# Performer attention and two expert layers on one core: attention's products in float32 on halves of the matrix array, two pairs of heads at a time

## The chip, the cores and the metric

The kernel runs on one core of one Trainium2 chip. The core has a matrix engine (PE; its weight loads are shown as PEld), a vector engine (DVE), a scalar engine (ACT), a general engine (POOL) and a queue engine (SP) that issues the transfers. The metric is the time of one execution on the device, in microseconds (us), lower is better: 965.58 us, the median of 3 runs (965.34 to 966.15).

## The reference

Four batches, 8 heads, 576 positions, 64 values per head; 128 random features `omega`. The attention is linear (features instead of a softmax over positions), then two expert layers follow, each with 2304 tokens of 512 values.

```python
def phi(x):                                    # x is q or k, scaled
    proj = np.einsum('bhsd,md->bhsm', x, omega)
    h = proj - np.sum(x * x, axis=-1, keepdims=True) / 2.0
    h = h - np.max(h, axis=-1, keepdims=True)
    return np.exp(h) / np.sqrt(m)
kv = np.einsum('bhsm,bhsd->bhmd', k_p, v)      # key sums
z = np.sum(k_p, axis=2)
num = np.einsum('bhsm,bhmd->bhsd', q_p, kv)    # numerators
den = np.einsum('bhsm,bhm->bhs', q_p, z)[..., None] + 1e-06
attn = num / den
# layer 1: silu(x @ w_gate) * (x @ w_val) @ w_out;  layer 2: squared, clipped (x @ w_in) @ w_out
```

## The kernel before

The program is written by a planner (`Planner`): each piece of work is a coroutine that yields operations (`Op`) with an engine and an assumed cost, waits for events, and takes buffers from rings. The planner walks through this in assumed time and emits the instructions; each engine runs its own in that order, and semaphores keep the dependencies. Where an operation may run on more than one engine, `pl.pick` takes the one that is free first by the plan. PE, DVE and ACT instructions of different coroutines are so interleaved by priorities (`PR_K`, `PR_Q`, `PR_C` and others).

There are eight PSUM banks of 128x512 (`bank`). Precision is that of float32: the expert layers write each operand as a high and a low part in a rounded format (`parts`, L411) and multiply three times (`split3`, L415 to 418). Attention does its products in one of two ways. In full float32 one product is two instructions on PE. In the split form an operand's high and low part are made by DVE, ACT or POOL, and a product is three instructions.

- Keys come in 36 groups (`k_group`) of two tiles of 128 positions, for a pair of heads. The pair's 64 values each stand above each other on the 128 rows of the array, and `omr` (128x256) is `omega` twice, on the diagonal, with zeros elsewhere. `front` (L620) makes the squares (`squares`), the projection, the maximum over 128 features, and the exponent. The first 26 key groups and the first 17 query groups (`NATP`) use float32 (L632), the others `split3` with `xhl` and `omh`, `oml`.
- Key sums (L705): for each tile and head one product of the 128 features with 128 columns: 64 values and 64 columns of ones, so that the sum `z` stands 64 times. `kv_evac` brings them to SBUF, as `kvr` in float32, and as `kvz` in two parts.
- Queries come in nine blocks of 256 positions and four pairs of heads (`q_group`). The features are transposed on PE (L790) to `qtn` or, split, to `qt` (L802). `num` multiplies: the first three blocks (`NATK`) in float32 on column halves of the array (L894), two heads side by side, numerators and denominators in one bank; the others split (L902). `norm_whole` and `norm_halves` divide: DVE transposes the denominators in 32x32 blocks, takes reciprocals of one column, and transposes back (L819 to 827, L838 to 860).
- The result `os` becomes a tile `x1s` in two parts (`x1_split`) and goes to DRAM. Expert steps of layer 1 begin when both halves of a block are there. Weights arrive as 64-bit numbers and are converted by one ACT and four DVE operations each (`to_f32`, L433 to 440), 68 of them in all.

A bank is returned when the last reader of it has been planned; a coroutine that asks for a bank waits in the plan.

Of the kernel before, what the change touches and what calls it, by code (L numbers as in the profile page):

```python
# [28 lines left out]
P = 128  # L29
# [15 lines left out]
SLACK_A = 0.0  # L45

O_OFF, P_OFF, H_OFF = 32, 48, 48

NATK = 3

SQ3 = True

NATP = 26

N_2 = 0

NWL, NB1 = 7, 8
KINS, VINS, QINS, EBK, EBQ, N_QT = 3, 5, 2, 4, 2, 3
N_KL, N_VL = 3, 0
# [10 lines left out]
PR_K0, PR_K, PR_Q0, PR_Q = 0.32, 1.04, 0.17, 0.83  # L70
PR_C0, PR_C, PR_CS = 0.66, 1.20, 1.10
# [4 lines left out]
N_GATE, N_CS = 2, 3  # L76
# [206 lines left out]
def performer_moe_kernel(ctx: ExitStack, tc: tile.TileContext, qG, kG, om, ident,  # L283
# [59 lines left out]
    stat = ring(att, "st", 10, [P, 4, 4])  # L343
    rec = ring(att, "rec", 2, [P, TB])
    rect = ring(att, "rect", 1, [P, TB // 32, 33])
    vin = ring(att, "vi", VINS, [P, 576])
    qts0 = ring(att, "qtn", 3, [P, 2, TB])
    qts = ring(att, "qt", N_QT, [P, 2, 2, TB], F32R)
    ids = att.tile([P, P], F32, name="ids")
    omr = att.tile([P, 256], F32, name="omr")  # L350
    omh = att.tile([P, 256], F32R, name="omh")
    oml = att.tile([P, 256], F32R, name="oml")
    pad(att, "pada", 64)
    ebufs = {False: ring(att, "ebk", EBK, [P, 512]), True: ring(att, "ebq", EBQ, [P, 512])}
    kin = ring(att, "ki", KINS, [P, 512])
    qin = ring(att, "qi", QINS, [P, 512])
    nat_b = sorted({b for b in range(4) for k in range(NATK) if b * 576 < (k + 1) * TB and k * TB < (b + 1) * 576})
    kvr = {(b, d): att.tile([P, 2, 2, P], F32, name=f"kvr{b}_{d}") for b in nat_b for d in range(2)}
    xhl = ring(att, "xhl", 2, [P, 2, 256], F32R)
    kvz = [[att.tile([P, 2, 2, 2, P], F32R, name=f"kvz{b}_{d}") for d in range(2)] for b in range(2)]  # L360
# [21 lines left out]
    lend(kin, "kl", N_KL, [P, 512])  # L382
    lend(vin, "vl", N_VL, [P, 576])
    lend(qin, "ql", 2, [P, 512])
    lend(ebufs[False], "el", 2, [P, 512])
# [194 lines left out]
    q_done = {(k, d): Ev() for k in range(NBLK) for d in range(2)}  # L580
# [3 lines left out]
    omr_ready, om_ready, ids_ready = Ev(), Ev(), Ev()  # L584

    def prep():
        yield from dma(omr, om, 131072)
        yield Op("ACT", c_act(256), lambda: nc.scalar.activation(omr, omr, AF.Copy, scale=scale))
        pl.set(omr_ready)
        yield Op("ACT", c_act(256), lambda: nc.scalar.activation(omh, omr, AF.Copy))  # L590
        yield Op("DVE", c_dve(256), lambda: nc.vector.tensor_tensor(out=oml, in0=omr, in1=omh.bitcast(F32), op=ALU.subtract))
        pl.set(om_ready)
        yield from dma(ids, ident, 65536)
        pl.set(ids_ready)

    def squares(x, sq, x_ev):

        if x_ev is not None:
            yield x_ev
        how = pl.pick(ACT=0.96, DVE=c_act(256) + c_dve(256))  # L600
        if how == "ACT":
            def acc4():
                for u in range(4):
                    xu = x[:, u * 64:(u + 1) * 64]
                    nc.scalar.activation(xu, xu, AF.Square, scale=0.25, accum_out=sq[:, u:u + 1])
            yield Op("ACT", 0.96, acc4)
        else:
            yield Op("ACT", c_act(256), lambda: nc.scalar.activation(x, x, AF.Square, scale=0.25))
            yield Op("DVE", c_dve(256), lambda: nc.vector.tensor_reduce(
                out=sq, in_=x.rearrange("p (u d) -> p u d", u=4), axis=AX.X, op=ALU.add))  # L610

    def margin():
        if moe_on.done and SLACK_A:
            yield SLACK_A
# [247 lines left out]
    def num(k, p, q_t):  # L862
# [53 lines left out]
        if q_cnt[k, d] < 2:  # L916
            return
# [829 lines left out]
```

## Time and profile before

| what | value |
|---|---|
| median of 3 runs | 965.58 us (965.34 to 966.15) |
| the profiled execution | 963.52 us |
| its span | 961.7 us |
| PE busy | 945.6 us (98%) |
| DVE busy | 824.1 us (86%) |
| ACT busy | 567.1 us (59%) |
| POOL busy | 96.8 us (10%) |
| PE clock granted | 1.00 |

The span is what the trace covers from the first to the last instruction; the execution's own time is 1.8 us longer. Busy time counts from an instruction's start to its end, and PE's instructions overlap by some 0.16 us, so the distance between two starts tells what one costs. Idle time of an engine that nothing waits for costs nothing.

### The profile page before, as it was taken

The page shows a single profiled execution, that of the slowest core. Times are in us where ns is not written, and L with a number is a line of the kernel's source. Part 1 is how long each engine was busy: PE and PEld are TensorE (multiplying, and loading weights), DVE is VectorE, ACT ScalarE, POOL GpSimd, SP SyncE. Part 2 cuts the span into 40 slices and gives each one's busy share as a digit, 9 for nine tenths or more (in the row PEclk, how much of TensorE's full clock was granted, in tenths as well). Part 3 has the DMA queues.
Part 4 walks back from the last instruction along what each step waited for, and adds up shares of the span by engine and source line. Part 5 has one row for each costly group of instructions (what it writes and reads, how often), then busy time and mean ns, then how long its engine had stood idle before and what let it go on. Part 6 is the DMA issues. An engine that isn't in the chain of part 4 may idle for free.

```text
span 961.7 us, 21166 instructions
## 1 busy us (share of the span) xinstructions
PE 945.6 (98%) x8094; PEld 927.5 (96%) x8094; DVE 824.1 (86%) x1695; ACT 567.1 (59%) x1490; POOL 96.8 (10%) x99
## 2 busy tenths in 40 slices
PE   8999999999999999999989999999999999999998
PEld 7789899999999999999989999999999999999998
DVE  7999899888999999999989999999889768867553
ACT  8999788887755545455544466564545455544331
POOL 0322246533300000000000000000000000000000
PEclk9999999999999999999999999999999999999999
DMA  8765646645478556574666583336423041303022
GB/s 301 253 198 183 200 154 219 197 140 173 166 241 256 161 190 207 189 248 153 198 206 220 173 277 123 116 125 232 126 73 122 1 143 45 132 1 111 1 89 88
DMA packets 90677, 154.67 MB, mean 161 GB/s; under 512 B 8528, under 2 KB 42320, under 8 KB 90576
## 3 DMA queue, kind: packets, MB, share of 16 engines
q1 hardware_dynamic: 90576, 153.32, 48.7%
q8 instruction: 63, 1.03, 0.4%
q14 instruction: 38, 0.31, 0.1%
HBM read 110.30 MB, written 42.99 MB: 159 GB/s over the span
## 4 chain that ended last, share of the span: by engine, by line
PE 64%; DVE 9%; DMA 7%; ACT 5%; issue 2%; SPq 1%; DVEq 0%; ACTq 0%
PE bank L416 21%; PE bank L418 20%; PE bank L417 20%; DMA ws<-in_w_dram 2%; DMA ws<-in_wo_dram 2%; DMA xq<-x1d 2%; PE bank L902 1%; SPq L390 1%; DVE x1s L409 1%; DMA wtr<-w32o 1%; PE bank L705 1%; PE bank L790 1%; DVE wt L440 1%; ACT rec L838 1%; DVE wt L438 1%
## 5 line engine op out<-in xcount | busy, mean ns | idle before, releaser
L416 PE MATMUL bank<-x1s,w 128*128 128x256 f32 x492 | 138.3, 281 | 0.7 <-DVE eb L1318 0.6
L417 PE MATMUL bank<-x1s,w 128*128 128x256 f32 x492 | 136.2, 277 | 0.0
L418 PE MATMUL bank<-x1s,w 128*128 128x256 f32 x492 | 136.2, 277 | 0.0
L416 PEld LDWEIGHTS bank<-x1s,w 128*128 128x128 f32 x492 | 92.5, 188 | 1.2 <-DVE eb L1318 0.8
L417 PEld LDWEIGHTS bank<-x1s,w 128*128 128x128 f32 x492 | 92.5, 188 | 0.0
L418 PEld LDWEIGHTS bank<-x1s,w 128*128 128x128 f32 x492 | 92.4, 188 | 0.0
L397 ACT ACTIVATE x1s<-xq 128x512 fp32r<-128x512 f32 x81 | 50.8, 628 | 56.0 <-DVE xq L409 27.9
L416 PE MATMUL bank<-x1s,wx 128*128 128x256 f32 x278 | 77.4, 279 | 4.0 <-ACT eb L397 2.6
L416 PE MATMUL bank<-x1s,wb 128*128 128x256 f32 x286 | 79.2, 277 | 0.0
L418 PE MATMUL bank<-x1s,wb 128*128 128x256 f32 x286 | 79.0, 276 | 0.0
L417 PE MATMUL bank<-x1s,wb 128*128 128x256 f32 x286 | 79.0, 276 | 0.0
L418 PE MATMUL bank<-x1s,wx 128*128 128x256 f32 x278 | 76.9, 277 | 0.0
L417 PE MATMUL bank<-x1s,wx 128*128 128x256 f32 x278 | 76.8, 276 | 0.0
L433 ACT ACTIVATE wt<-ws 128x512 f32<-128x512 f32 x68 | 45.8, 676 | 43.9 <-DMA ws<-in_w_dram 22.8
L409 DVE TENSOR_TENSOR x1s<-xq,x1s 128x512 fp32r<-128x512 f32 x90 | 61.4, 684 | 8.4 <-ACT x1s L397 8.1
L397 ACT ACTIVATE eb<-bank 128x512 f32<-128x512 f32 x95 | 55.9, 589 | 19.7 <-PE bank L418 19.3
L397 ACT ACTIVATE hlr<-hb 128x512 fp32r<-128x512 f32 x53 | 33.5, 632 | 49.8 <-PE bank L417 35.2
L416 PEld LDWEIGHTS bank<-x1s,wx 128*128 128x128 f32 x278 | 52.2, 188 | 4.8 <-ACT eb L397 3.3
L651 DVE TENSOR_REDUCE st<-bank 128x4 f32<-128x512 f32 x72 | 48.7, 684 | 8.7 <-PE bank L632 3.9
L416 PEld LDWEIGHTS bank<-x1s,wb 128*128 128x128 f32 x286 | 53.7, 188 | 0.1
L418 PEld LDWEIGHTS bank<-x1s,wb 128*128 128x128 f32 x286 | 53.7, 188 | 0.0
L417 PEld LDWEIGHTS bank<-x1s,wb 128*128 128x128 f32 x286 | 53.7, 188 | 0.0
(281 smaller groups left out, 3610.0 us busy)
## 6 DMA issues: line engine op xcount, KB each, us to landing
ws<-in_w_dram SPq DMA_DIRECT2D x40, 512.0 KB, 4.8
ws<-in_wo_dram SPq DMA_DIRECT2D x28, 512.0 KB, 5.1
xq<-x1d SPq DMA_DIRECT2D x36, 256.0 KB, 5.0
xq<-x2d SPq DMA_DIRECT2D x36, 256.0 KB, 4.1
qi<-in_qG_dram SPq DMA_DIRECT2D x34, 256.0 KB, 3.1
ki<-in_kG_dram SPq DMA_DIRECT2D x33, 256.0 KB, 3.6
vi<-in_kG_dram SPq DMA_DIRECT2D x28, 192.0 KB, 3.5
x1d<-os SPq DMA_DIRECT2D x18, 256.0 KB, 3.2
```

The costliest lines, as they stand in the source:

```text
L390: yield Op("SP", 0.06, lambda: nc.sync.dma_start(dst, src))
L397: yield Op("ACT", c_act(n), lambda: nc.scalar.activation(dst, src, AF.Copy, scale=1.0 if scale is None else scale))
L409: yield Op("DVE", c_dve(n), lambda: nc.vector.tensor_tensor(out=dst, in0=a, in1=b, op=op), True)
L416: nc.tensor.matmul(ps, l_hi, r_hi, start=first, stop=False, skip_group_check=shared)
L417: nc.tensor.matmul(ps, l_hi, r_lo, start=False, stop=False, skip_group_check=shared)
L418: nc.tensor.matmul(ps, l_lo, r_hi, start=False, stop=last, skip_group_check=shared)
L433: yield Op("ACT", 0.575, lambda: nc.scalar.activation(t, hw.bitcast(F32), AF.Abs))
L438: yield Op("DVE", c_dve(512), lambda: nc.vector.scalar_tensor_tensor(out=ti, in0=lw, scalar=29, in1=ti, op0=ALU.logical_shift_right, op1=A ...
L440: yield Op("DVE", c_dve(512), lambda: nc.vector.scalar_tensor_tensor(out=ti, in0=hw, scalar=0xC0000000, in1=ti, op0=ALU.bitwise_and, op1=A ...
L651: yield Op("DVE", c_dve(512), lambda: nc.vector.tensor_reduce(out=st[:, :, 0], in_=psv, axis=AX.X, op=ALU.max, negate=True))
L705: nc.tensor.matmul(kp[:, 2 * pr + a], e[:, u * P:(u + 1) * P], vb[:, vi + (dv if li == 4 else 0), a * 64:a * 64 + P], start=(li == 0 and a ...
L790: nc.tensor.transpose(tp[:, (a * 2 + t) * P:(a * 2 + t + 1) * P], e[:, u * P:(u + 1) * P], ids)
```

## The change

All products of attention are full float32, and the parts of operands (`xhl`, `omh`, `oml`, `kvz`, the two layers of `qt`) are gone. Keys are taken in five groups per batch, one of a single old group and four of two (`GROUPS`), queries two pairs of heads at a time, 18 groups.

- Projections: `omega` stands twice, on rows 0 to 63 and on rows 64 to 127. Each head of a pair is a product of 64 rows on its own half, with its own bank, alternating. 
- Key sums: the 128 features are cut into two halves of 64, each written to its half of the bank's partitions, with 65 columns (64 values and one of ones). `kv_evac` spreads that one column over 64 when it copies.
- Numerators and denominators: always on column halves, for two pairs of heads in one call, in two banks. One `norm` of 512 columns takes the place of `norm_whole` and `norm_halves`.
- Two banks are taken together (`bank_pair`), by one coroutine at a time. Loads are cut into two halves; values are loaded with 130 columns a tile instead of 192. Priorities and ring sizes change.

The number of instructions that the engines get changes so: PE 7354 rows to 7579, DVE 1685 to 1531, ACT 989 to 879. The diff, cut to its core:

```diff
-KINS, VINS, QINS, EBK, EBQ, N_QT = 3, 5, 2, 4, 2, 3
-N_KL, N_VL = 3, 0
+KINS, VINS, QINS, EBK, EBQ, N_QT = 3, 5, 2, 6, 4, 3
+N_KL, N_QL, N_EL = 2, 1, 2
+
+GROUPS = ((0,), (1, 2), (3, 4), (5, 6), (7, 8))
...
+    halves = slice(0, 64), slice(64, P)
+
+    def bank_pair():
+
+        tok = yield Get(two_banks)
+        b0 = yield Get(bank)
+        b1 = yield Get(bank)
+        pl.put(two_banks, tok)
+        return b0, b1
...
+    def front(xb, n, loads, is_q, res, rng):
 
         st = yield Get(stat)
...
-            def proj():
-                for t in range(2):
-                    nc.tensor.matmul(ps[:, t * 256:(t + 1) * 256], xt[:, t * P:(t + 1) * P], omr, start=True, stop=True)
-            yield from margin()
-            yield Op("PE", 0.86, proj)
...
-            yield from parts(hl[:, 0], hl[:, 1], xt, 256)
...
-            def proj():
-                for t in range(2):
-                    split3(ps[:, t * 256:(t + 1) * 256], hl[:, 0, t * P:(t + 1) * P], hl[:, 1, t * P:(t + 1) * P],
-                           omh, oml, True, True)
...
+        banks = yield from bank_pair()
+
+        def proj():
+            for u in range(2 * n):
+                for a, h in enumerate(halves):
+                    nc.tensor.matmul(banks[a][:, u * P:(u + 1) * P], xb[h, 0, u * P:(u + 1) * P], omr[h], start=True, stop=True,
+                                     skip_group_check=True)
+        yield Op("PE", 0.446 * n + 0.1, proj)
...
+        pv = [ps[:, 0:256 * n].rearrange("p (u m) -> p u m", m=P) for ps in banks]
+        for a in range(2):
+            yield Op("DVE", c_dve(256 * n), lambda: nc.vector.tensor_reduce(
+                out=sv[:, a, units, 0], in_=pv[a], axis=AX.X, op=ALU.max, negate=True))
...
-                        nc.tensor.matmul(kp[:, 2 * pr + a], e[:, u * P:(u + 1) * P],
-                                         vb[:, vi + (dv if li == 4 else 0), a * 64:a * 64 + P],
...
+        def mm():
+            for kp, v, u, pr, li in todo:
+                for a in range(2):
+                    for m, h in enumerate(halves):
+                        nc.tensor.matmul(kp[h, 2 * pr + a, 0:65], es[a][:, u * P + 64 * m:u * P + 64 * m + 64],
+                                         v[:, 65 * a:65 * a + 65], start=(li == 0 and a == 0),
+                                         stop=(li == 8 or (li == 4 and pr == 0)), skip_group_check=True)
+        yield Op("PE", 0.232 * len(todo) + 0.15, mm)
...
     def kv_evac(b, d):
         kb = kv_bank.pop((b, d))
...
+        yield from copy(kz[:, :, 0:64], kp[:, :, 0:64], 256, False, 1.0 / P)
+        yield from copy(kz[:, :, 64:P], kp[:, :, 64:65].to_broadcast([P, 4, 64]), 256, False, 1.0 / P)
         pl.put(bank, kb)
-        pl.set(kv_split[b, d])
...
-                yield Op("DVE", c_dve(512), lambda: nc.vector.tensor_tensor(out=lv, in0=tp, in1=hv.bitcast(F32), op=ALU.subtract))
...
+        x = yield Get(osb)
         rc = yield Get(rec)
...
+        banks = yield from bank_pair()
 
         def mm():
...
+            for r in range(2):
+                for what in range(2):
+                    for b, c0, c1 in cuts:
+                        for a, h in enumerate(halves):
+                            nc.tensor.matmul(banks[what][h, r * TB + c0:r * TB + c1], kvr[b, d][:, r, a, halves[what]],
+                                             q_t[:, r, a, c0:c1], start=True, stop=True, skip_group_check=True)
```

The start of PE's order before, after the warm-up. `ki`, `kl` are keys, `qi` queries, `vi` values, `ebk` and `ebq` the exponentials, `ids` the identity:

```order
L632 MATMUL bank_63<-omr,ki_157 128x256 x2
L632 MATMUL bank_64<-omr,ki_158 128x256 x2
L632 MATMUL bank_65<-omr,ki_159 128x256 x2
L632 MATMUL bank_66<-omr,kl_175 128x256 x2
L632 MATMUL bank_67<-omr,kl_176 128x256 x2
L632 MATMUL bank_69<-omr,qi_160 128x256 x2
L632 MATMUL bank_70<-omr,qi_161 128x256 x2
L632 MATMUL bank_68<-omr,kl_177 128x256 x2
L705 MATMUL bank_63<-vi_135,ebk_151 128x128 x4
```

The same place now, the first rows of each group:

```order
L625 MATMUL bank_63<-omr,ki_155 128x128
L625 MATMUL bank_64<-omr,ki_155 128x128
...
L625 MATMUL bank_65<-omr,ki_156 128x128
L625 MATMUL bank_66<-omr,ki_156 128x128
...
L625 MATMUL bank_67<-omr,ki_157 128x128
L625 MATMUL bank_68<-omr,ki_157 128x128
...
L690 MATMUL bank_66<-vi_135,ebk_145 64x65 x2
L690 MATMUL bank_66<-vi_135,ebk_146 64x65 x2
```

A projection of 256 columns in one bank has become products of 128 columns that alternate between two banks, one for each head; a key sum of 128 partitions has become two of 64.

DVE's order before, in the mixed stage, where two numerators of a split block are divided (`rec` holds denominators, then reciprocals; `st` small columns):

```order
L845 STREAM_TRANSPOSE rect_134<-rec_132 128x8x32
L846 RECIPROCAL st_129<-rect_134 128x8
L848 STREAM_TRANSPOSE rec_132<-st_129 128x256
L399 CAST xhl_167<-qi_161 128x256
L845 STREAM_TRANSPOSE rect_134<-rec_133 128x8x32
L802 TENSOR_TENSOR qt_144<-bank_65,qt_144 128x512
L846 RECIPROCAL st_127<-rect_134 128x8
L802 TENSOR_TENSOR qt_143<-bank_70,qt_143 128x512
L848 STREAM_TRANSPOSE rec_133<-st_127 128x256
L748 SCALAR_TENSOR_TENSOR kvz_1_169<-bank_63,kvz_1_169 128x512
L853 TENSOR_TENSOR os_102<-bank_64,rec_133 64x256
```

And now, one division in the same stage:

```order
L781 STREAM_TRANSPOSE rect_134<-bank_70 128x16x32
L635 TENSOR_REDUCE st_128<-st_128 128x8
L418 TENSOR_SCALAR wt_78<-wt_78 128x512
L783 TENSOR_REDUCE st_124<-rect_134 128x16
L647 TENSOR_TENSOR ebk_150<-bank_66,st_128 128x512
L785 RECIPROCAL st_124<-st_124 128x16
L420 TENSOR_SCALAR wt_78<-wt_78 128x512
L786 STREAM_TRANSPOSE rec_132<-st_124 128x512
L631 TENSOR_REDUCE st_130<-bank_64 128x4
L790 TENSOR_TENSOR os_104<-bank_63,rec_132 128x512
```

The transposes read PSUM directly and are twice as long, and the low parts of `qt`, `xhl` and `kvz` no longer stand between them.

## Rows read from the trace of the kernel before

**Rows 1.** The page, busy time, share of the span and instructions of each engine.
```profile
PE 945.6 (98%) x8094; PEld 927.5 (96%) x8094; DVE 824.1 (86%) x1695; ACT 567.1 (59%) x1490; POOL 96.8 (10%) x99
```

**Rows 2.** Table by stage: stretch, its length, busy us (instructions) by engine, clock, DMA.
```profile
0.00:47.30 47.30, 43.21 (x260) 34.88 (x261) 39.15 (x122) 43.25 (x209) 8.74 (x13) 1.00 0.83 281
47.30:256.10 208.80, 206.18 (x1729) 198.47 (x1728) 185.91 (x472) 175.12 (x644) 83.35 (x83) 1.00 0.57 183
256.10:640.00 383.90, 378.12 (x3306) 376.26 (x3305) 364.38 (x693) 203.91 (x382) 4.66 (x4) 1.00 0.59 192
640.00:961.70 321.70, 318.05 (x2807) 317.85 (x2805) 234.69 (x410) 144.83 (x258) 0.00 (x0) 1.00 0.28 91
```

**Rows 3.** First x1 product, last split numerator: ns min/median/max, first and last start.
```profile
L416 PE MATMUL bank<-x1s,w x492: 276/276/469, 47.3 to 924.9; 128*128 128x256 f32 x164
...
L902 PE MATMUL bank<-qt,kvz x192: 213/276/364, 113.5 to 256.0; 128*128 128x256 f32 x96, 128*128 128x128 f32 x48, 128*128 128x192 f32 x24, 128*128 128x64 f32 x24
```

**Rows 4.** Matrix engine's timeline, float32: start us, us, line, operation, instructions.
```profile
31.28 1.95 PE L705 MATMUL bank<-vi,ebk 128*128 128x128 f32 x16
33.06 1.03 PE L632 MATMUL bank<-omr,ki 128*128 128x256 f32 x4
33.93 1.05 PE L705 MATMUL bank<-vi,ebk 128*128 128x128 f32 x8
```

**Rows 5.** The same at two visits to the column halves; PEld are loads.
```profile
27.05 0.61 PE L705 MATMUL bank<-vi,el 128*128 128x128 f32 x4
27.59 1.95 PE L894 MATMUL bank<-qtn,kvr 128*64 128x256 f32 x16
29.47 0.66 PE L790 MATMUL bank<-ids,ebq 128*128 128x128 f32 x4
...
63.57 0.76 PEld L894 LDWEIGHTS bank<-qtn,kvr 128*64 128x64 f32 x16 [0.17 <-DVE ebk L663]
...
63.57 1.10 PE L894 MATMUL bank<-qtn,kvr 128*64 128x64 f32 x16
64.61 0.70 PE L632 MATMUL bank<-omr,qi 128*128 128x256 f32 x2
```

**Rows 6.** The same, split products of 256 columns one by one.
```profile
700.05 0.28 PE L418 MATMUL bank<-x1s,wx 128*128 128x256 f32 x1
700.16 0.28 PE L416 MATMUL bank<-wb,hlr 128*128 128x256 f32 x1
```

**Rows 7.** Groups up to 262 us: count, busy us, mean ns, idle before.
```profile
L651 DVE TENSOR_REDUCE st<-bank 128x4 f32<-128x512 f32 x72 | 48.7, 684 | 8.7 <-PE bank L632 3.9 <-PE bank L418 2.6 <-PE bank L705 0.8
L654 DVE TENSOR_REDUCE st<-st 128x4 f32<-128x8 f32 x144 | 18.8, 148 | 0.5
L838 ACT ACTIVATE rec<-bank 64x256 f32<-64x256 f32 x48 | 18.2, 379 | 9.0 <-PE bank L902 6.3 <-issue 1.2 <-ACT wt L433 0.7
L802 DVE TENSOR_TENSOR qt<-bank,qt 128x512 fp32r<-128x512 f32 x24 | 16.3, 677 | 3.1 <-ACT qt L397 3.0
L407 POOL TENSOR_TENSOR xhl<-qi,xhl 128x256 fp32r<-128x256 f32 x19 | 13.9, 741 | 24.5 <-ACT xhl L397 15.0 <-DVE xhl L399 9.4
L848 DVE STREAM_TRANSPOSE rec<-st 128x256 f32<-128x256 f32 x24 | 10.6, 441 | 0.6
L845 DVE STREAM_TRANSPOSE rect<-rec 128x256 f32<-128x256 f32 x24 | 10.5, 437 | 3.8 <-ACT rec L838 3.7
L853 DVE TENSOR_TENSOR os<-bank,rec 64x256 f32<-64x256 f32 x24 | 10.1, 419 | 0.7
L858 ACT ACTIVATE os<-bank 64x256 f32<-64x256 f32 x24 | 9.0, 377 | 0.3
L407 POOL TENSOR_TENSOR xhl<-ki,xhl 128x256 fp32r<-128x256 f32 x9 | 7.2, 801 | 19.9 <-ACT xhl L397 18.4 <-DVE xhl L399 1.0 <-DVE rect L845 0.5
L397 ACT ACTIVATE xhl<-qi 128x256 fp32r<-128x256 f32 x17 | 7.1, 418 | 1.2 <-PE bank L417 1.0
L397 ACT ACTIVATE xhl<-ki 128x256 fp32r<-128x256 f32 x8 | 3.4, 433 | 0.0
```

More of the change, by code (lines that the diff above doesn't have):

```diff
@@ L579, in performer_moe_kernel @@
     kv_ready = {k: Ev() for k in kvr}
-    q_done = {(k, d): Ev() for k in range(NBLK) for d in range(2)}
+    two_banks = Ring([0])
     x1_tile = {}
@@ new lines, in expo, with each @@
+        def expo(a):
+            e, ps = es[a], banks[a]
+            if pl.pick(ACT=2 * n * 0.262, DVE=c_dve(256 * n)) == "ACT":
+                def each():
+                    for u in range(2 * n):
+                        nc.scalar.activation(e[:, u * P:(u + 1) * P], ps[:, u * P:(u + 1) * P], AF.Exp, bias=sv[:, a, u, 3:4])
+                yield Op("ACT", 2 * n * 0.262, each)
+                pl.put(bank, ps)
+            else:
+                yield Op("DVE", c_dve(256 * n), lambda: nc.vector.tensor_tensor(
+                    out=e[:, 0:256 * n].rearrange("p (u m) -> p u m", m=P), in0=pv[a],
+                    in1=sv[:, a, units, 3].unsqueeze(2).to_broadcast([P, 2 * n, P]), op=ALU.add))
+                pl.put(bank, ps)
+                yield Op("ACT", c_act(256 * n), lambda: nc.scalar.activation(e[:, 0:256 * n], e[:, 0:256 * n], AF.Exp))
@@ L717, in performer_moe_kernel @@
+        for u in range(2 * n):
+            i = 2 * gs[0] + u
+            if i % 9 == 8:
+                pl.spawn(kv_evac(b, i // 9), pl.cur.prio - 0.1)
+        for e in es:
+            back(ebufs[False], e)
+        for g in gs:
+            back(vin, v_tile[b, g])
     v_ready = {(b, g): Ev() for b in range(4) for g in range(9)}
@@ L810, in q_group @@
-        pl.spawn(num(k, p, q_t), pl.cur.prio - 0.05)
-    halves = slice(0, 64), slice(64, P)
-    def norm_whole(ps, pb, rc, xr):
+                    for t in range(2):
+                        u = 2 * r + t
+                        nc.tensor.transpose(tp[:, (a * 2 + t) * P:(a * 2 + t + 1) * P], es[a][:, u * P:(u + 1) * P], ids)
+            yield Op("PE", 4 * 0.11, trans)
+            left[0] -= 1
+            if left[0] == 0:
+                for e in es:
+                    back(ebufs[True], e)
@@ L816, in norm_whole, with norm @@
+            yield from copy(q_t[:, r].rearrange("p a t -> p (a t)"), tp, 512, False)
+            pl.put(bank, tp)
+        ends = [pl.spawn(turn(r), pl.cur.prio) for r in range(2)]
+        for ev in ends:
+            yield ev
+        pl.spawn(num(k, d, q_t), pl.cur.prio - 0.05)
+    def norm(pn, pd, rc, x):
         tt = yield Get(rect)
         st = yield Get(stat)
-        s8 = st.rearrange("p a b -> p (a b)")
-        yield Op("DVE", 0.36, lambda: nc.vector.transpose(out=tt[:, :, 0:32], in_=ps[:, 1].rearrange("p (n c) -> p n c", c=32)))
```

396 lines of the change are left out of this document (123 added, 273 removed).

## The prediction

> **What bounds the kernel now.** I read the busy line of the page first, then a table by stage, then the matrix engine's own timeline at three places, then the groups of the other engines. The busy line gives the matrix engine 98% of the span and the vector engine 86% [rows 1]; a mean does not say which of them ends last where, so the table by stage decides [rows 2]. I cut it at the first expert product, 47.3 us, and at the last attention product, 256.0 us [rows 3]. Up to 47.3 us matrix, vector and scalar engine are all nearly full (43.2, 39.2 and 43.3 us of 47.3), and nothing but attention runs on the matrix engine. From 47.3 to 256.1 us attention and the first expert steps are mixed: the matrix engine is busy 206.2 of 208.8 us, the vector engine 185.9, the scalar engine 175.1. From 256.1 us on there is expert work only: until 640 us the vector engine is at 364.4 of 383.9 us and the matrix engine idles 5.8 us, later only the matrix engine counts. The change touches the first two stages, so what it is worth is read there: matrix time taken out, as long as the vector engine lets it go.
>
> A busy time hides that matmuls overlap, so prices are distances between starts. A float32 product of 256 columns (two instructions) gives 33.06 to 33.93, 0.87 us for 4, 0.217 each; one of 128 columns gives 31.28 to 33.06, 1.78 us for 16, 0.111 each [rows 4]. A split product's instruction of 256 columns takes 0.11 to 0.12 [rows 6]; I use 0.113.
>
> **The change part by part: the matrix engine.** Before, per instruction:
> - projections: 43 groups in float32, 4 x 0.217 = 0.87 each, 37.3 us; 29 groups split, 6 x 0.113 = 0.68 each, 19.7 us. Together 57.0.
> - key sums: 80 tile products of two heads, two instructions each, 320 x 0.111 = 35.5 us.
> - numerators: 12 calls in float32 on column halves and 24 split ones of 6 or 12 instructions. Two float32 calls in a row, 27.59 to 29.47, take 1.88 us for 16 instructions of 256 columns [rows 5]: 8 pairs at 0.217 are 1.73, so the two halves run side by side and 0.15 is lost on the way in and out. 0.94 x 12 = 11.3, a little more for the cut ones: 12.5. The split ones are 192 instructions x 0.113 = 21.7.
> - transposes: the same 144 on both sides.
> Sum without the transposes: 126.7 us.
>
> After:
> - key sums: 640 instructions of 65 columns, in 320 pairs on column halves. The cut numerator call [rows 5] holds the same thing: 63.57 to 64.61 is 1.04 us for 4 pairs of 192 columns and 4 of 64; take off 0.15 and 4 x 0.16 for 192 columns (0.217 x 3/4) and 0.25 is left, 0.06 a pair. 320 x 0.06 = 19 us, 16 less.
> - numerators: 18 calls of 8 pairs at 0.217, 31.2 us without the way in and out, against 34.2: 3 less.
> - projections: 576 instructions of 128 columns in 288 pairs on row halves. No row of before shows row halves. Between 0.111 a pair (side by side, as the column halves) and 0.222 (one after the other) lies 32 to 64 us. I take 0.111, by the nearest row, which is the column halves': 25 less than 57.
> - changes of tiling: in the order of instructions the engine changes between whole array, row halves and column halves 83 times, before 16 times. A visit to the column halves costs 0.15 inside and about 0.1 ahead of it (the 4 products of 27.05 need 0.44, the next starts after 0.54) [rows 5], 0.25 for two changes. Not counting what is in the 12.5 above: 83 x 0.125 = 10.4. A change straight from row to column halves is not shown; 0 to 0.25 for each of these 23 keeps this term between 7.5 and 13.
> Sum: 19 + 31.2 + 32 + 10.4 = 92.6; 34 us less, between 2 (halves one after the other) and 37.
>
> One rule speaks against the 0.111. Loads of 64 columns come 16 in 0.76 us in the cut call [rows 5], less than 0.05 from load to load, with products running beside. The Trainium skill, "TensorE: Matmul & The Clock Gate", section "LDWEIGHTS (loading the stationary operand)", puts a load at its columns divided by 1.2 in nanoseconds, some 53 for 64 columns, 0.85 us for 16 one after another: the trace's 0.76 says that column halves load side by side. For two row halves the same page would give 107 each, 0.213 a pair if one path carried both. By that the projections would be 61 us and nearly the whole gain of this term gone; by the trace's behaviour on column halves it is 32. That is one of the rivals below.
>
> **The other engines.** Vector engine, to the end of attention [rows 7]: out go the low parts of the transposed queries (24 x 0.677 = 16.3), the half-block norms' transposes and products (10.5 + 10.6 + 10.1) with their 24 reciprocals, the 12 whole norms (two transposes at 0.44 and 8 products at 0.42 among them, some 18 in all), 6 low parts of key sums (4 at 0.68 each). In come 18 norms of 512 columns: two transposes at about 0.71 (0.441 plus 256 columns at the 0.265 that separates 0.419 from 0.684), 16 products at 0.68 and 0.3 of small ones, together 42. The small reductions go from 144 to 76 (-10 at 0.148), the exponent's subtraction on this engine from 27 to 38 (+7.5 at 0.68), the sums of squares grow by 4. Net about -29 us. The scalar engine loses the denominators' and numerators' halves (18.2 + 9.0) and the projections' high parts (7.1 + 3.4 at least), 38 us and more; POOL loses the low parts (13.9 + 7.2). Neither was ahead of the vector engine after 47 us, so I count their gains at nothing.
>
> **Where it lands.** Up to the first expert product attention has to bring the keys of one batch and two blocks of queries through the scalar engine, and this part was float32 before too: its squares and exponentials by head are the same. So the first expert product stays at 47 to 50 us. The matrix engine needs only about 28 us there now (a third of the pairs are ahead of it in the order) against 41: these 13 us turn into idle time. From there 80 us of attention are left instead of 102, 22 less, and the order leaves 33 expert instructions (3.7 us) for later that stood before the end of attention: 256.1 - 22 - 3.7 + 2 (later first product) = 232. By the vector engine: 225.1 us up to 256.1 [rows 2], a share of 88%. Minus 29, plus 11 for five more weight conversions that the order now has ahead of the end of attention (30 against 25, two passes of 0.68 and two near 0.44 each), is 207; at the same share 235, and some 4 us of expert work moved behind takes it to 231. The two answers agree on 232. Behind it: 705.6 + 3.7 - 3 (of the 5.8 us of idle matrix time before 640 us, since five conversions fewer are left where the vector engine is at 95%; 0 to 5.8) = 706.3. Span 938.3. The profiled execution took 963.5 us with a span of 961.7, so 940.1; it lay 2.1 us under the median of the runs shown, which may or may not recur. I forecast 939.
>
> What is late next: in the first 50 us the scalar engine, then vector and matrix engine together. Added waits: a projection and a numerator now need two free banks of eight at once, and a token lets one of them gather at a time; queued behind a waiting projection on the matrix engine is the next expert product, whose own bank is held too. The visible idle time of that stage is 2.6 us [rows 2]; I take no more than that, and 0 to 38 us as its bounds (the slower rival below). Loads are no term: the values shrink from 192 to 130 columns a tile, and the transfers' share is 0.57 in that stage.
>
> **Rivals.**
> - All of the matrix time comes out. If the first 47 us shrink with it, nothing turns idle: 961.7 - 34 - 5 = 923 span, 925. Against: the scalar engine's 43.3 of 47.3 us. Range 924 to 931. 0.10.
> - The vector engine holds the mixed stage: groups twice as large come in bursts, two maxima of 0.684 in a row [rows 7], and the matrix engine runs out of expert products to fill in. 10 to 22 us of the saving lost: 950 to 962. For: a vector share of 88% with no slack shown; against: the expert products. A pair of 65 columns that costs 0.11 instead of 0.06 (+16 us, 955) falls in here too. 0.12.
> - The row halves run one after the other. A third of the 32 us falls into the idle time of the first stage, two thirds come back: 939 + 21 = 960, 955 to 966. For: no row shows them, and the rule on loads; against: column halves load and run side by side. It decides from about 0.2 us a pair. 0.07, of which 0.03 within the bound of no change. It is also what remains if the change does not do what it says.
> - Slower: the second bank. 38 projections and 18 numerators each ask for two banks at once, and a bank comes free after a pass of the vector engine over it, 0.684 us for 512 columns [rows 7], or later where it is the second of two. With one such wait on the matrix engine each time, 56 x 0.684 = 38 us are added: 977. It decides from 0.47 us a time (26 us over 56), where the gain against the median is gone. For: a projection's two banks are held through maximum, sums and exponent, before it was one. Against: the 2.6 us of visible idle time in the mixed stage, and expert products queued between. 0.06.
> - The forecast: 931 to 950, likeliest 939. 0.65.
>
> **How the numbers follow.** Faster by over 0.2% (about 1.9 us, what a measurement of this kernel can tell from no change): 0.65 + 0.10 + 0.12 + 0.04 = 0.91. Within: 0.03. Slower: 0.06. The range of 8 in 10: its lower end 925 is the rival with everything out, its upper end 957 takes in half of the one on the vector engine; the other half, the row halves in a row and the slower one stay outside, 0.19 in all.
>
> **What would show it.** Row-half products in pairs a few ns apart, 0.11 from pair to pair, is the step with most weight; 0.22 there makes the forecast wrong. 65-column pairs at 0.06. The first expert product between 45 and 52 us with the matrix engine idle 10 us and more ahead of it. The last attention product at 225 to 240 us. Behind it 700 to 708 us. A vector engine below 80% with matrix idle time in the mixed stage, ended by waits on banks, would speak for the second rival.

## The result, and the profile after

The changed kernel takes 950.96 us (median of 4 runs, 948.91 to 953.10), the kernel before beside it 965.46 (964.20 to 966.15): a ratio of 0.986 [0.984, 0.988], 14.5 us faster. The forecast was 939, range 925 to 957. The profiled execution took 949.58 us, its span is 947.8 us; the sum behind the forecast had 940.1 and 938.3. So 9.5 us of span are to be found.

The page's busy line of the kernel after, to be laid beside [rows 1]:

```profile
PE 920.2 (97%) x8708; PEld 892.9 (94%) x8708; DVE 799.7 (84%) x1536; ACT 515.2 (54%) x1226; POOL 67.6 (7%) x58
```

The first expert product and the last attention product, columns as in [rows 3], and the table by stage cut there, columns as in [rows 2]:

```profile
L400 PE MATMUL bank<-x1s,w x492: 276/276/388, 53.0 to 911.0; 128*128 128x256 f32 x164
...
L817 PE MATMUL bank<-qt,kvr x384: 219/378/687, 23.2 to 239.4; 128*64 128x256 f32 x96, 128*64 128x64 f32 x32, 128*64 128x192 f32 x32, 128*64 128x128 f32 x32
```
```profile
0.00:53.00 53.00, 40.09 (x508) 31.08 (x508) 45.29 (x110) 45.85 (x184) 11.10 (x14) 0.90 0.82 273
53.00:239.40 186.40, 180.32 (x2057) 164.36 (x2059) 161.77 (x340) 126.39 (x419) 53.88 (x42) 1.00 0.64 206
239.40:640.00 400.60, 395.65 (x3464) 393.50 (x3461) 380.24 (x722) 208.46 (x387) 2.60 (x2) 1.00 0.59 190
640.00:947.80 307.80, 304.12 (x2684) 303.92 (x2682) 212.39 (x366) 134.53 (x238) 0.00 (x0) 1.00 0.23 76
```

Against [rows 2] the mixed stage has lost 22.4 us (208.8 to 186.4), the first stage has become 5.7 us longer (47.3 to 53.0), and what lies behind attention 2.8 us longer (705.6 to 708.4, with 3.7 us of expert products moved there). The first stage's matrix engine idles 12.9 us instead of 4.1; the clock it was granted there is 0.90 of full speed, before 1.00.

The matrix engine's timeline in that stage, where [rows 4, 5] stand for before (start us, us, line, operation, instructions, idle before it and what ended it):

```profile
12.75 3.52 PE L625 MATMUL bank<-omr,qi 64*128 64x128 f32 x32 [3.62 <-DMA qi<-in_qX_dram]
16.20 3.04 PE L690 MATMUL bank<-vi,ebk 128*64 128x65 f32 x88
19.17 2.06 PE L625 MATMUL bank<-omr,kl 64*128 64x128 f32 x32
...
25.04 1.16 PE L625 MATMUL bank<-omr,qi 64*128 64x128 f32 x16
26.13 1.39 PE L690 MATMUL bank<-vi,ebk 128*64 128x65 f32 x40
27.44 1.16 PE L625 MATMUL bank<-omr,qi 64*128 64x128 f32 x16
...
33.08 1.41 PE L625 MATMUL bank<-omr,ki 64*128 64x128 f32 x14 [1.96 <-ACT kvr L381]
37.43 2.08 PE L625 MATMUL bank<-omr,ki 64*128 64x128 f32 x16 [2.94 <-ACT ebq L643]
```

At 25.04 sixteen row-half instructions take 1.09 us to the next start: 8 pairs and the way in and out. Forty of 65 columns take 1.31: 20 pairs, 0.06 each with a change of form. Both prices of the forecast are there. The waits, at 12.75 on a transfer of queries and at 33.08 and 37.43 on banks that the scalar engine still reads, are not what the forecast had priced.

### The profile page after: what moved, and what is told of

It is laid out like the page before. It is cut to its first block, busy times and chain, and to the rows that moved or that the text cites. A ratio compares the mean times of both kernels' runs of the same rounds, so it can differ in the third digit from the quotient of the medians.

```text
span 947.8 us, 21783 instructions
## 1 busy us (share of the span) xinstructions
PE 920.2 (97%) x8708; PEld 892.9 (94%) x8708; DVE 799.7 (84%) x1536; ACT 515.2 (54%) x1226; POOL 67.6 (7%) x58
## 4 chain that ended last, share of the span: by engine, by line
PE 64%; DVE 11%; DMA 6%; ACT 2%; issue 2%; SPq 0%; DVEq 0%; ACTq 0%
PE bank L400 20%; PE bank L401 20%; PE bank L402 20%; DMA ws<-in_w_dram 2%; DMA ws<-in_wo_dram 2%; PE bank L817 2%; DVE x1s L393 1%; PE bank L625 1%; DVE w L393 1%; DVE wt L424 1%; DVE wt L422 1%; DVE hb L1211 1%; PE bank L763 1%; DVE wb L393 1%; DVE xi L393 1%
## 5 line engine op out<-in xcount | busy, mean ns | idle before, releaser
L400 PEld LDWEIGHTS bank<-x1s,wx 128*128 128x128 f32 x278 | 52.2, 188 | 1.4 <-ACT eb L381 1.2
L402 PEld LDWEIGHTS bank<-x1s,wx 128*128 128x128 f32 x278 | 52.2, 188 | 0.8 <-POOL wx L391 0.8
```

Of the source, the lines that this page charges most:

```text
L400: nc.tensor.matmul(ps, l_hi, r_hi, start=first, stop=False, skip_group_check=shared)
L402: nc.tensor.matmul(ps, l_lo, r_hi, start=False, stop=last, skip_group_check=shared)
```

## The experiments

All but the last keep the changed kernel's order of instructions on every engine, apart from what is added, left out or turned round inside a group. The kernel before was run beside each; its medians were 964.1 to 965.6. Times are medians; rows and stages are those of one profiled execution of each kernel.

**The row halves in turn.**

```
-            for u in range(2 * n):
-                for a, h in enumerate(halves):
+            for a, h in enumerate(halves):
+                for u in range(2 * n):
```

> The projections of a group run through one row half first and then through the other, so that neighbouring products share a half and cannot lie beside each other; the order on every other engine is that of the changed kernel. Theory A (row halves lie side by side, and matrix time is what the mixed stage is made of): from start to start 0.11 us for each single product instead of for a pair, 32 us more work; a third of it falls into the idle time of the first 53 us, 20 us and more do not: 970 to 980 us. Rival B (the vector engine holds the mixed stage, matrix time is slack): 951 to 957 us. Rival C (the halves load one after the other anyway and gain nothing): no change, 950 to 952 us.

960.66 us (959.60 to 962.31), 9.7 more than the changed kernel; ratio to before 0.995 [0.993, 0.997]. The same visit as at 25.04, from its timeline, and its stages:

```profile
122.72 1.71 PE L625 MATMUL bank<-omr,ki 64*128 64x128 f32 x16
```
```profile
0.00:57.20 57.20, 47.49 (x509) 37.49 (x509) 46.54 (x110) 46.53 (x183) 11.19 (x14) 0.88 0.76 253
57.20:251.70 194.50, 190.59 (x2059) 175.42 (x2059) 163.07 (x340) 127.26 (x419) 53.36 (x42) 1.00 0.61 197
```

It takes 1.64 us to the next start, at 124.36, against 1.09. Inside one half the single starts are 0.112 us apart, as far as the pairs are when the halves alternate: a product alone costs what a pair costs, so the row halves do run side by side. Alternating is not all or nothing, though. Where the second half follows the first, three products of each still start in pairs, 4 to 6 ns apart, in 19 of the 21 visits of this length that stand alone in the trace: 13 steps of 0.112 instead of 16. Some 120 of the 288 pairs are left in this way, so not 32 but about 19 us of matrix time are added. The matrix engine is busy 17.5 us more (937.7), 7.4 in the first stage and 10.3 in the mixed one; the stages are longer by 4.2 and 8.1, since a part fits into idle time. For both reasons no expectation met it.

**The projections on the whole array**, each head's `omega` beside 64 rows of zeros:

```
-                    nc.tensor.matmul(banks[a][...], xb[h, 0, ...], omr[h], ...
+                    nc.tensor.matmul(banks[a][...], xb[:, 0, ...], omz[:, a], ...
```

> The projections go over the whole array again, each head against omega with zeros on the other head's rows, in the same two banks and the same order. Theory A: 576 instructions at 0.111 are 64 us instead of 32, but the 27 visits to the row halves, at about 0.25 to 0.3 us each, are gone: 24 us more, of which some 8 in the idle first stage: 963 to 970 us, under the kernel with the halves in turn by about 8 us. Rival (changes of tiling cost nothing that shows): equal to the kernel with the halves in turn, 970 to 980 us. Rival B (matrix time is slack): 951 to 957 us.

964.68 us (962.60 to 967.79), 13.7 more, ratio 0.999 [0.998, 1.001]: without row halves the whole change is worth nothing that can be measured. The matrix engine is busy 21.3 us more (941.5), and the time lies in the 963 to 970 of theory A. Sixteen instructions take 1.95 us:

```profile
76.51 1.95 PE L630 MATMUL bank<-omz,ki 128*128 128x128 f32 x16
```

**The key sums on the whole array**, 128 features by 65 columns:

```
-                    for m, h in enumerate(halves):
-                        nc.tensor.matmul(kp[h, 2 * pr + a, 0:65], es[a][:, u * P + 64 * m:u * P + 64 * m + 64], ...
+                    nc.tensor.matmul(kp[:, 2 * pr + a, 0:65], es[a][:, u * P:(u + 1) * P], ...
```

> The key sums keep their 65 columns, but each is one product with all 128 features on the whole array instead of two of 64 on column halves. Theory A (the gain of the key sums is that of the columns, 65 instead of 128, and a load of 128 columns keeps up): 0.06 us from start to start, the same work, and up to 20 visits to the column halves fewer at 0.25 us: 946 to 950 us. Rival (a load of 128 columns takes as long as 128 columns of product, 0.11 us, so the halves are what makes 65 columns pay): 320 x 0.05 = 16 us more, 10 to 15 of them behind the first stage: 960 to 967 us.

967.99 us (961.11 to 970.65, 10 runs), 17.0 more, ratio 1.002 [0.999, 1.005].

```profile
127.00 1.89 PE L689 MATMUL bank<-vi,ebk 128*128 128x65 f32 x16
```

Sixteen instructions of 65 columns on the whole array take 1.8 us to the next start, 0.112 each, as much as those of 128 columns: the columns do not set the pace. The Trainium skill, "TensorE: Matmul & The Clock Gate", section "LDWEIGHTS (loading the stationary operand)", puts a load at its columns divided by 1.2 in nanoseconds, 107 for 128 columns; by that the load sets it, and the 0.112 here agrees. The ten runs differ mostly by the clock: 961.11 at a mean clock of 0.994, 970.65 at 0.984. So some of the 17 us is clock, and the expectation of 960 to 967 is met only by the runs above 0.986.

**The column halves in turn.**

```
+            for m, h in enumerate(halves):
                 for kp, v, u, pr, li in todo:
                     for a in range(2):
-                    for m, h in enumerate(halves):
```

> The loop over the two column halves goes outermost in the key sums: first all products of a group on one half, then all on the other; the same 640 pairs of instructions, the same forms and visits. If the two halves work side by side in the changed kernel (two instructions that start 7 ns apart every 0.055 us), 640 instructions of 0.05 us each go from half to whole: 16 us more for the matrix engine, of which about half comes out as with the projections in turn (17.5 us more busy, 9.7 us more time): 957 to 962. If the matrix engine overlaps them in this order too, or a load of 64 columns and not the 65 columns sets the pace: 950 to 953.

958.61 us (957.62 to 961.84), 7.7 more, ratio 0.994 [0.993, 0.996], as expected; the matrix engine is busy 13.7 us more. The visit of 40 instructions:

```profile
128.80 2.32 PE L690 MATMUL bank<-vi,ebk 128*64 128x65 f32 x40
```

To the next start, at 131.05, it is 2.25 us against 1.31: here too the gain hangs on the alternation, and here too three pairs are left where one half follows the other.

**The maxima over half the features.**

```
-                out=sv[:, a, units, 0], in_=pv[a], axis=AX.X, op=ALU.max, negate=True))
+                out=sv[:, a, units, 0], in_=pv[a][:, :, 0:64], axis=AX.X, op=ALU.max, negate=True))
```

> The maximum is taken over 64 of the 128 features and an absolute value stands in for the exponential, so the result is not attention; the order on every engine is unchanged, and only the vector engine's maxima become shorter, 0.68 to about 0.42 us for 68 of 76, some 18 us in all. Theory B (the vector engine holds the first stage and what is lost in the mixed one): the first expert product 3 us earlier and more, the mixed stage shorter by 5 and more: 938 to 945 us. Theory A (matrix work, changes of tiling and the scalar engine's start hold it): 948 to 952 us.

949.03 us (947.59 to 952.78), the same time. Its mixed stage:

```profile
53.90:240.10 186.20, 180.09 (x2059) 164.17 (x2059) 151.84 (x340) 126.59 (x419) 53.59 (x42) 1.00 0.63 206
```

The vector engine has 9.9 us less to do there and the stage lasts 186.2 us, as the changed kernel's 186.4 with 161.77: it does not hold the mixed stage. Nor did the 5 us taken from it in the first stage bring the first expert product earlier (53.9).

**One visit cut into four, and its control.** A product of one column on the whole array (`small`) is added behind each of the tile products of the key sums, or, in the control, all of them behind the visit.

```
         for kp, v, u, pr, li in todo:
             for a in range(2):
                 ...
+            small(kp, v, u)          # the control: in a loop of its own behind this one
```

> Adds 80 products of one column on the whole array to the key sums, one behind every four (of 320) pairs' products, into a column that nothing reads: each visit to the column halves is cut into four or five, 80 visits instead of 20. To be compared with the kernel that has the same 80 products, all at the end of the 20 visits. If a visit costs 0.25 us of the matrix engine, and this engine sets the time in the stage where attention and expert layers are mixed: 60 x 0.25 = 15 us of work, of which half to all comes out in time: 8 to 15 us more than the kernel beside it. If the change of form is hidden: less than 3 us more than it.

> The 80 products of one column, all behind the key sums' visit of their group: 20 visits as before. By itself 80 x 2 x 0.06 to 0.11 us = 10 to 18 us of work for the matrix engine, of which half to all comes out: 956 to 969.

989.82 us (988.04 to 993.88), the control 967.59 (965.39 to 969.97): 22 us for 60 more visits, more than the 8 to 15 expected. The two timelines:

```profile
121.92 0.45 PE L694 MATMUL bank<-vi,ebk 128*64 128x65 f32 x8
122.30 0.38 PE L687 MATMUL bank<-vi,ebk 128*128 128x1 f32 x2
122.61 0.45 PE L694 MATMUL bank<-vi,ebk 128*64 128x65 f32 x8
```
```profile
124.40 1.15 PE L694 MATMUL bank<-vi,ebk 128*64 128x65 f32 x32
125.48 1.05 PE L687 MATMUL bank<-vi,ebk 128*128 128x1 f32 x8
```

Cut, a tile product with its small one takes 0.69 us from start to start; in the control it is about 0.45 (a quarter of 1.08 - 0.15 for the way in and out, and two times 0.11). So a visit costs 0.24 us, two changes of 0.12, and the 60 visits 14.5 us of matrix time. The time rose by 7 us more than that. The clock fell with it: the three runs of 988.04 to 990.2 had a mean granted clock of 0.983 or 0.984, the control's runs 0.989 to 0.994, and 5 to 11 thousandths of this span are 5 to 11 us of matrix time. No run separated the two.

**The clock of the start.** Eight products of zeros fill the waits on the matrix engine, four ahead of the first query projection and two ahead of each of two key projections.

```
         def proj():
+            for _ in range(fill):
+                nc.tensor.matmul(banks[0], idle[:, 0:P], idle, start=True, stop=True)
```

> Eight more products of zeros (128x512, float32, 0.86 us each at full clock) stand in the start, four ahead of the first query projection and two each ahead of two key projections, where the matrix engine waits for a transfer and for banks; the order of all other instructions is that of the changed kernel. Theory B (the half clock costs time): the granted clock of the start stays at or near 1.00, mean 0.998 or more, and the time falls by 3 to 5, to 946 to 948. Theory A (scalar and vector engine hold the start, so a slower matrix engine there costs nothing): clock up, time 949 to 952. If the fillers are in the way: 952 to 954.

954.57 us (954.13 to 957.42), 3.6 slower. Its timeline:

```profile
8.70 3.70 PE L624 MATMUL bank<-hb 128*128 128x512 f32 x8
12.69 1.16 PE L627 MATMUL bank<-omr,qi 64*128 64x128 f32 x16 [0.29 <-DMA qi<-in_qX_dram]
...
15.24 2.79 PE L692 MATMUL bank<-vi,ebk 128*64 128x65 f32 x88
17.96 2.19 PE L627 MATMUL bank<-omr,kl 64*128 64x128 f32 x32
...
37.09 3.26 PE L624 MATMUL bank<-hb 128*128 128x512 f32 x4 [3.42 <-ACT ebq L645]
40.28 1.52 PE L627 MATMUL bank<-omr,ki 64*128 64x128 f32 x16
```

The clock stayed full up to 36 us, and the key sums started 1.0 us earlier than in the changed kernel (15.24 against 16.20), the next projection 1.2 (17.96 against 19.17). At 37.09 the bank came 0.3 us earlier than at 37.43 there. The rest had gone into a longer wait on the scalar engine: a faster matrix engine is worth next to nothing up to there. The last two fillers stood behind that wait instead of in it, ran mostly at half clock (3.26 us for what takes 1.98 at 30 us) and pushed the projection from 37.43 to 40.28 and the first expert product from 53.0 to 55.9; that is the loss. What the half clock costs behind that wait, from 37 us on, this kernel does not show: it fell there here too (0.72 from 36 to 42 us, against 0.61).

**Transfers or engines, and both.** Three kernels. One leaves out the sums of squares. One keeps them but drops the second copy of keys and queries, which only they use, and takes them of the first copy. One leaves out both. The sum of squares is subtracted from the exponent's argument and added back with the maximum, so it only affects the rounding.

```
-                        nc.scalar.activation(xu, xu, AF.Square, ...)      # no squares
-        return [pl.spawn(dma(xb[:, l, ...], src[:, l], ...), ...) for l in range(2)]
+        return [...]                                                      # one copy: l == 0 alone
```

> Leaves out the sums of squares in attention (the scalar engine's squares and the vector engine's reductions of them); in the exponent's argument the sum of squares is subtracted and then, with the maximum, added back, so that the argument is the same up to rounding. The order on every engine is that of the changed kernel with these instructions missing. To the first expert product this takes 28 us of work from the scalar engine (21.5 with accumulators, 6.5 without) and 6.4 us from the vector engine. Theory A (scalar and vector engine together hold the start): the first expert product comes at 43 to 47 us instead of 53.0, the waits for banks in the start go, and the time is 939 to 945. Theory B (what the start lost is the matrix engine's half clock, and the engines do not hold it): only the idle gaps that let the clock fall get shorter, 946 to 950. Theory C (the transfers hold the start, which are busy 0.97 and more from 6 to 30 us): first product stays at 52 to 54 us, 949 to 952.

> Every group of keys and queries is loaded once instead of twice (the second copy, with positions on the partitions, is used by the squares alone); the squares are taken of the first copy instead, so that they are other numbers, and cancel in the exponent's argument as before. All instructions of the engines and their order stay; only these transfers are missing, some 3.2 MB of the 14.5 MB moved ahead of the first expert product (273 GB/s over 53.0 us). Theory C (transfers hold the start): the first expert product comes at 45 to 50 us, since 3.2 MB take 8 to 10 us at the 310 to 380 GB/s of the start, and below some 47 us the 45 to 46 us of scalar and vector work hold; time 944 to 948. If transfers hold nothing (theory A, or the order of waits on the matrix engine): first product at 52 to 53.5, time 949 to 952.

> The second copies and the sums of squares are both left out (the squares cancel in the exponent's argument up to rounding), in the changed kernel's order on every engine. Without squares alone the first expert product came at 52.4 us. Theory C together with A (transfers first, engines next): 41 to 46 us, time 937 to 943. C without A: as with one copy alone, 945 to 948. If neither holds the start but the matrix engine's own order and its waits for banks: 51 to 53, 946 to 949.

| kernel | first expert product | time | ratio to before |
|---|---|---|---|
| changed kernel | 53.0 | 950.96 | 0.986 [0.984, 0.988] |
| no squares | 52.4 | 947.34 | 0.983 [0.981, 0.985] |
| one copy | 53.6 | 948.07 | 0.982 [0.980, 0.984] |
| neither | 47.3 | 941.39 | 0.976 [0.974, 0.977] |

The first stage of the three, in that order:

```profile
0.00:52.40 52.40, 39.04 (x509) 30.24 (x509) 40.21 (x100) 30.43 (x77) 11.75 (x24) 0.90 0.83 275
```
```profile
0.00:53.60 53.60, 40.53 (x508) 30.24 (x508) 45.95 (x110) 46.19 (x183) 11.12 (x14) 0.94 0.62 195
```
```profile
0.00:47.30 47.30, 38.71 (x509) 29.04 (x509) 40.34 (x100) 30.24 (x77) 11.90 (x24) 0.96 0.70 220
```

Fifteen us less of scalar work (the expectation's 28 added up instructions that overlap) and five less of vector work, and the first expert product comes 0.6 us earlier. A quarter fewer bytes (195 GB/s over 53.6 us, 10.5 MB, against 14.5), and it comes no earlier. Both together, and it comes 5.7 us earlier (47.3, where the expectation had 41 to 46; its time was right). By their times the first two are not clear of the changed kernel, for the intervals of their ratios overlap its own; the third is. The start has two limits of nearly the same length, so that taking one away shows the other; an experiment on one of them alone would have called it harmless. Without squares the other one can be seen: the scalar engine waits until 35.62 for a weight whose transfer was issued at 28.94 among the others, the exponents stand behind it in its order, and the matrix engine waits for their bank. Scalar engine's and matrix engine's timeline of that kernel:

```profile
35.62 0.66 ACT L419 ACTIVATE wt<-ws 128x512 f32<-128x512 f32 x1 [2.10 <-DMA ws<-in_w_dram]
36.19 0.61 ACT L383 ACTIVATE w<-wt 128x512 fp32r<-128x512 f32 x1
36.71 3.18 ACT L643 ACTIVATE ebq<-bank,st 128x128 f32<-128x128 f32 x12
```
```profile
37.88 2.08 PE L625 MATMUL bank<-omr,ki 64*128 64x128 f32 x16 [6.26 <-ACT ebq L643]
```

The same projection with one copy, and with neither:

```profile
36.56 2.08 PE L625 MATMUL bank<-omr,ki 64*128 64x128 f32 x16 [2.96 <-ACT ebq L643]
```
```profile
32.16 2.28 PE L625 MATMUL bank<-omr,ki 64*128 64x128 f32 x16 [3.90 <-ACT ebq L643]
```

It starts at 37.43 in the changed kernel; from it to the first expert product there are 14 to 17 us in all four. So what the two together gain is gained ahead of this wait, where the matrix engine stands idle for the scalar engine. The clock, which is higher as well (0.96 against 0.90), does not explain it.

My theories A (engines) and C (transfers) were each wrong alone. By its time, 947.34, the kernel without squares alone would have spoken for B (946 to 950). B (the clock) is put aside by the fillers and by these starts up to this wait; what half clock costs behind it stays open. The matrix engine's own work is no free term in the start either: the halves in turn, 7.4 us more of it there, moved the first expert product to 57.2.

**Planned anew.** As the last kernel, without the two small reductions that took the squares off and on, and with the planner's own new order.

> As the kernel without second copies and squares, and besides without the two small reductions per group that subtracted and added the squares back, with the order on all engines planned anew for what is left. It has all that the result needs, the squares cancelling up to rounding. If the changed kernel's fixed order keeps some of the gain: first expert product at 36 to 42 us, time 928 to 938; if not, as the kernel with the old order, 937 to 943; worse than that only if the new order happens to serve the mixed stage badly.

941.29 us (939.98 to 945.01), ratio 0.976 [0.974, 0.978]: not better than with the old order. It and the kernel with neither are the fastest of this study, 24 us under the kernel before. Its stages:

```profile
0.00:42.40 42.40, 37.13 (x524) 28.92 (x524) 35.64 (x72) 33.45 (x100) 7.14 (x12) 1.00 0.75 237
42.40:223.40 181.00, 177.17 (x2041) 163.09 (x2043) 146.98 (x266) 112.93 (x291) 56.46 (x44) 1.00 0.60 193
223.40:640.00 416.60, 409.15 (x3553) 404.96 (x3550) 383.21 (x724) 213.74 (x392) 2.60 (x2) 1.00 0.56 182
```

The start is 4.9 us shorter again and attention ends at 223.4 instead of 231.9. The same expert work stands behind attention in both (6148 instructions), but it takes 714.8 us instead of 707.4: the matrix engine idles 7.5 us up to 640, where the kernel with the old order idled 3.7, and its products stand less close. What the start gave was handed back behind attention; which waits of the new order do it stays open.

## Why the prediction was right, and where it was wrong

**The number: inside the range, in part by luck.** The gain was forecast at 26.5 us and came out at 14.5. The 950.96 lies 12 us above the forecast and just outside the 931 to 950 that carried it; the range took it in only because it reached up into the rival on the vector engine, which is not what happened.

**The pairs on row halves, 0.111 each: right.** Without them (13.7 us more) nothing is left of the gain. The key sums' halves weigh no less (17.0 us more, a part of it clock). The Trainium skill, "TensorE: Matmul & The Clock Gate", section "LDWEIGHTS (loading the stationary operand)", read for one path, gave an estimate of 0.213 a pair; the measured pair decides. Inside one half the 0.112 from start to start agrees with that rule, but 128 columns of product cost about as much, so no run says which of the two sets it there. The rival with halves in turn was priced at 21 us more; measured, it costs 9.7, since its order leaves some 120 pairs side by side and its 17.5 us of matrix time fall partly into idle time.

**Key sums at 0.06 a pair: right**, 26.13 to 27.44 with 20 pairs. **Changes of form at 0.125: right**, by the cut visits and their control.

**"So the first expert product stays at 47 to 50 us": wrong, 53.0.** The step counted what stands ahead of the first expert product for the matrix engine (a third of the pairs) and kept the other engines' old sum. In groups of one old size, the maxima's rows tell how many stand ahead (line, count, busy us, mean ns, idle before); first before, up to 47.3 us, then after, up to 53.0 us:

```profile
L651 DVE TENSOR_REDUCE st<-bank 128x4 f32<-128x512 f32 x21 | 14.0, 683 | 3.1 <-PE bank L632 2.8
```
```profile
L631 DVE TENSOR_REDUCE st<-bank 128x4 f32<-128x512 f32 x22 | 14.6, 687 | 0.0
...
L631 DVE TENSOR_REDUCE st<-bank 128x2 f32<-128x256 f32 x4 | 1.6, 422 | 5.0 <-PE bank L625 5.0
```

21 groups before, 22 and 4 halves, 24, after. At 47.3/21 = 2.25 us a group 24 take 54 us, close to the 53.0 that came; no run took the three groups out, so this is reckoned and not shown. Vector work rose from 39.15 to 45.29 us, scalar work from 43.25 to 45.85, bytes from 13.3 to 14.5 MB (281 and 273 GB/s by the length). "Loads are no term" was read from the mixed stage; in the start they are one of the two limits. The miss is 3.7 us against the 49.3 in the sum. The vector engine's sum up to the end of attention was right (45.29 + 161.77 = 207.1 us against 207); only its split was not. The "about 28 us" of the matrix engine was wrong too: it was busy 40.1. By the forecast's own prices, the instructions that the trace has ahead of the first expert product make 33 us (96 pairs of projections 10.7, 108 of key sums 6.5, 32 of numerators 6.9, 32 transposes 3.6, 15 changes of form 1.9, the warm-up 3.8), and some 10 us of the stage ran at half clock (the six-us rows at the end). That it idled 12.9 us there, near the 13 forecast, is luck: the stage was longer.

**The mixed stage: 186.4 us against 182.7 in the sum.** The matrix engine idles 6.1 us there, before 2.6 [rows 2]; the sum had no idle time added, and these 3.5 us are nearly the whole miss. The two largest waits after, and the only one of a projection (waited for, us in total, times, longest):

```profile
PE bank L400 <- ACT qt L381: 1.7, 1, 1.7
PE bank L400 <- DVE hb L910: 1.4, 1, 1.4
...
PE bank L625 <- DVE hb L915: 0.4, 1, 0.4
```

Single waits, each on another buffer. The rival that had the vector engine hold this stage (950 to 962) contains the measured time, but not for its reason: with 9.9 us of vector work gone the stage kept its length. The slower rival wanted 0.47 us or more at each of 56 projections and numerators; one projection with 0.4 us and no numerator waits here, which puts it aside too. The waits on two banks are in the start, some 5 us, on the scalar engine.

**Behind attention: 708.4 against 706.3.** The 3.7 us moved there came; of the 3 us of idle time that should have gone, 0.8 did (9.4 to 8.6 us, length less busy). Together 3.7 + 3.7 + 2.1 = 9.5 us, the whole miss of the span. Of the 12 us to the median, 1.4 more lie between the profiled execution and the median, and 1.1 between the sum's 940.1 and the forecast of 939.

## What to carry to other kernels

Two halves of the matrix array work side by side where their instructions alternate in the order; with one half first, three pairs a visit are left of it. A visit to the halves between products on the whole array costs a quarter of a microsecond, so long visits with alternating halves are the form to write. When a change takes time from one engine in a stage that several limits share, count the work of all of them that stands ahead of the stage's end, bytes too, in the new order: here three more groups on top of 21 stood ahead of the first expert product, and it came later by about what they weigh. And to learn what holds such a stage, take away the suspects together as well as one by one.

## What the runs showed of the hardware

- The matrix engine's granted clock fell to half, 1.2 of 2.4 GHz, twice in the start of the changed kernel; the kernel before had 1.00 there, and the kernel planned anew as well. In six-us stretches of the changed kernel:

```profile
6.00:12.00 6.00, 2.57 (x36) 2.19 (x34) 5.37 (x15) 3.51 (x21) 0.00 (x0) 1.00 0.97 347
12.00:18.00 6.00, 5.25 (x84) 4.88 (x86) 5.51 (x12) 6.00 (x26) 0.00 (x0) 0.72 0.97 344
...
30.00:36.00 6.00, 2.26 (x24) 1.58 (x20) 5.29 (x13) 4.90 (x25) 4.25 (x3) 0.82 1.02 346
36.00:42.00 6.00, 4.54 (x32) 3.12 (x32) 5.76 (x14) 6.00 (x19) 1.42 (x2) 0.61 0.73 265
```

It fell behind a stretch with 2.6 us of matrix work in six, and within one with 2.3. Thirty-two row-half instructions took 3.45 us to the next start in one such stretch and 1.98 at full clock (12.75 and 19.17 in the timeline above). With the first gap filled by products of zeros the clock stayed at 1.00 up to 36 us.
- Two loads of 128 columns on the two row halves land within one 0.112 us, side by side, while on the whole array each takes that long; on column halves two of 64 columns come every 0.06 us. With all products of one half ahead of the other's, the pairs are gone but for three where the halves meet.
- Runs of one kernel differ by the clock: the kernel with whole key sums went from 961.1 to 970.7 us as its mean clock went from 0.994 to 0.984, some 0.9 us for each thousandth. In its trace the clock falls in the mixed stage too (0.98 there).
